# Low parts of half B's weights on VectorE, its conversions later in the order, and a list schedule that keeps GpSimd's arithmetic and VectorE's SBUF-only steps apart

## The chip, the cores and the metric

One core of a Trainium2 chip. The metric is the time of one execution on the device, in microseconds; the median of some runs counts. PE is TensorE, ACT is ScalarE, DVE is VectorE, POOL is GpSimd and SP is the engine that issues most DMAs.

## The reference

Attention over 4 batches and 8 heads of 576 x 64 with a threshold under the row's maximum, then two mixture layers on its 2304 x 512 output, with 2048 hidden units each:

```python
scores = scale * np.matmul(q, k.transpose(0, 1, 3, 2))
thresh = np.max(scores, axis=-1, keepdims=True) - tau
scores = np.where(scores >= thresh, scores, -1000000000.0)
attn = np.exp(scores - np.max(scores, axis=-1, keepdims=True))
attn = attn / (np.sum(attn, axis=-1, keepdims=True) + 1e-09)
x = np.matmul(attn, v)                    # -> 2304 x 512
h = x @ moe_w_in;  g = h * np.clip(h + 3.0, 0.0, 6.0) / 6.0
x = g @ moe_w_out
h = x @ moe2_w_in; g = h - np.tanh(h)
out = g @ moe2_w_out
```

The mixture weights arrive as 64-bit floats (two 32-bit words for a number), so the kernel converts them itself.

## The kernel before

The matrix products of the mixture layers run as three passes over pairs of a high and a low part (`mm3`: high x high, high x low, low x high). Every weight tile therefore goes through a conversion, `load_w` (L334 to L383): a DMA on SP brings 512 KB into one of three `st` buffers (L351 for the in-weights, L356 for the out-weights); ACT takes the absolute value of the upper words (L359) into `wu` (or, for half A, into a PSUM buffer `m`: the argument `scratch`); DVE does four steps on it, L362 and L364 (one input each), L367 and L370 (two inputs each, 128 x 512); then `hi_lo` (L385) writes the high part on ACT (L388) and the low part by a subtraction on GpSimd (L391). An in-weight has two such pairs of 128 x 256, an out-weight one of 128 x 512. The `st` buffer is free for the next load once the low parts have been computed.

The program's stages: attention, on PE interleaved with layer 1 of the first mixture, half A of its hidden units (`layer1`: 8 calls of 256 or 320 tokens, weights resident); then half B of the first mixture (`hidden` and `second`, 9 blocks of 256 tokens, 8 hidden tiles m each, from 511 us on), for which 16 weights are loaded and converted by `load_w` (L935 to L941) while the attention ends; then the second mixture in two halves. In the attention DVE does a row maximum L597, a threshold product L608 and steps on q and k (L507, L500); `invert` (L675 and L678) makes the reciprocals by which GpSimd scales the attention's output (L688), before PE transposes it (L685) and ACT and DVE (L694, L696) make its high and low part, `xT`. In layer 1 a gate is ACT L706, DVE L708, ACT L713 and the low part L716 (on GpSimd for layer 1, on DVE for half B); the second product is L749. In half B a matmul group is 12 matmuls of 128 x 256, h or m by `hidden` and ya by `second`. GpSimd also issues the loads of half B's x (L905).

What sets the order is `Plan` (L62 to L169), a list scheduler that runs when the kernel is built. Each task has an engine, a modelled duration, a key and the tasks that it depends on. In model time each free engine takes, of the tasks whose inputs are there and whose ring buffers have a slot, the one with the smallest key. The order found is the order of each engine's instruction queue; on the chip each engine then runs its queue in order and waits on semaphores. The weights of half B have the key `start - FW + WBO + WBS * (2 * m + o)` for the load and that plus 3 and further steps for the conversion, with `WBO` = 0 and `WBS` = 1.8.

```python
end = free[e] = now + t.dur
if t.xfer or e == "dma":
    end = moving = max(moving, now + 1.3) + t.xfer
```

## Time and profile before

| | |
|---|---|
| median of 3 runs | 1117.58 us (1115.91 to 1121.68) |
| the profiled execution | 1115.07 us |
| its span in the profile | 1113.3 us |
| its mean granted TensorE clock | 0.968 of full speed |
| PE busy in the span | 1045.2 us (94%) |
| DVE busy | 826.1 us (74%) |
| ACT busy | 660.0 us (59%) |
| POOL busy | 377.1 us (34%) |

Busy time counts an engine as long as an instruction is in it, so that a DVE instruction which is held up counts as busy too. Matmuls overlap each other, and their ends are modelled. In the timelines the number in brackets is the time for which the engine was idle ahead of the instruction, and the name behind it is what ended that idle time. A clock of 1.00 is TensorE's upper level of 2.4 GHz.

### The profile page before, as it was taken

The page shows a single profiled execution, that of the slowest core. Times are in us where ns is not written, and L with a number is a line of the kernel's source. Part 1 is how long each engine was busy: PE and PEld are TensorE (multiplying, and loading weights), DVE is VectorE, ACT ScalarE, POOL GpSimd, SP SyncE. Part 2 cuts the span into 40 slices and gives each one's busy share as a digit, 9 for nine tenths or more (in the row PEclk, how much of TensorE's full clock was granted, in tenths as well). Part 3 has the DMA queues.
Part 4 walks back from the last instruction along what each step waited for, and adds up shares of the span by engine and source line. Part 5 has one row for each costly group of instructions (what it writes and reads, how often), then busy time and mean ns, then how long its engine had stood idle before and what let it go on. Part 6 is the DMA issues. An engine that isn't in the chain of part 4 may idle for free.

```text
span 1113.3 us, 23731 instructions
## 1 busy us (share of the span) xinstructions
PE 1045.2 (94%) x8912; PEld 974.5 (88%) x8912; DVE 826.1 (74%) x1737; ACT 660.0 (59%) x1420; POOL 377.1 (34%) x413
## 2 busy tenths in 40 slices
PE   5668799999999999989899999999999999999998
PEld 4556788998999899979899999988989888888887
DVE  6889877688778876758676776896796786656653
ACT  6877888688868876555443444654564564333332
POOL 3666757566756675586211100000000010010100
PEclk8669899999999999999899999999999999999999
DMA  7889678867987787868797764654732662643613
GB/s 187 174 210 212 132 189 159 189 133 190 163 171 144 175 141 146 183 198 256 204 293 232 240 196 166 236 181 142 265 132 86 224 202 77 190 132 79 199 46 95
DMA packets 283666, 193.96 MB, mean 174 GB/s; under 512 B 203424, under 2 KB 254112, under 8 KB 283552
## 3 DMA queue, kind: packets, MB, share of 16 engines
q1 hardware_dynamic: 268672, 166.50, 57.5%
q0 software_dynamic: 14256, 25.69, 8.1%
q8 instruction: 70, 1.15, 0.4%
q10 hardware_dynamic: 624, 0.26, 0.1%
q14 instruction: 44, 0.36, 0.1%
HBM read 96.99 MB, written 52.95 MB: 135 GB/s over the span
## 4 chain that ended last, share of the span: by engine, by line
PE 79%; DVE 9%; ACT 4%; DMA 3%; issue 3%; POOL 1%; SPq 0%; DVEq 0%; ACTq 0%; POOLq 0%
PE ya L403 26%; PE m L403 21%; PE h L403 10%; PE s L592 7%; PE m L749 7%; PE tp L643 5%; DVE e L608 2%; PE tp L475 2%; DMA pt<-pp 1%; DVE z L597 1%; DMA st<-in_moe_w_in_dram 1%; ACT e L599 1%; ACT pp L613 1%; POOL pp L617 1%; DVE st L370 1%
## 5 line engine op out<-in xcount | busy, mean ns | idle before, releaser
L403 PE MATMUL ya<-wo,g 128*128 128x512 f32 x864 | 238.0, 395 | 0.6 <-ACT g L713 0.3
L617 POOL TENSOR_TENSOR pp<-e,pp 128x128 f16<-128x128 f32 (+3 forms) x160 | 185.4, 1179 | 119.7 <-ACT pp L613 62.6
L403 PEld LDWEIGHTS m<-x,wi 128*128 128x128 f32 x1392 | 187.3, 189 | 12.5 <-ACT t L1118 0.3
L403 PE MATMUL m<-x,wi 128*128 128x256 f32 x1392 | 194.6, 281 | 0.1
L403 PEld LDWEIGHTS ya<-wo,g 128*128 128x128 f32 x864 | 146.7, 188 | 19.8 <-DVE wu L1164 0.9
L597 DVE TENSOR_REDUCE z<-s 128x1 f32<-128x576 f32 x144 | 108.3, 753 | 51.5 <-PE s L592 50.5
L403 PEld LDWEIGHTS h<-x,wi 128*128 128x128 f32 x1008 | 136.1, 191 | 7.8
L403 PE MATMUL h<-x,wi 128*128 128x256 f32 x1008 | 142.1, 283 | 0.0
L713 ACT ACTIVATE g<-t 128x256 fp32r<-128x256 f32 x216 | 89.4, 415 | 75.6 <-DVE t L1131 49.5
L608 DVE SCALAR_TENSOR_TENSOR e<-s,z,e 128x576 f32<-128x576 f32 x144 | 116.1, 811 | 15.6 <-ACT e L599 10.0
L716 DVE TENSOR_TENSOR g<-t,g 128x256 fp32r<-128x256 f32 x216 | 94.8, 440 | 42.7 <-ACT g L713 38.2
L403 PE MATMUL m<-xT,ai 128*128 128x256 f32 (+1 forms) x768 | 120.8, 303 | 2.7 <-DVE t L708 1.5
L592 PE MATMUL s<-ks,q 128*128 128x288 f32 x512 | 105.1, 334 | 17.7 <-DVE e L608 17.1
L403 PE MATMUL ya<-g,wo 128*128 128x256 f32 x864 | 116.3, 284 | 3.8 <-DVE g L716 3.2
L599 ACT ACTIVATE e<-s,z 128x576 f32<-128x576 f32 x144 | 105.3, 738 | 23.1 <-DVE z L597 18.2
L1130 ACT ACTIVATE t<-t 128x256 f32<-128x256 f32 x128 | 53.4, 417 | 106.3 <-DVE t L1123 105.7
L403 PEld LDWEIGHTS ya<-g,wo 128*128 128x128 f32 x864 | 109.1, 192 | 4.7 <-DVE g L716 3.8
L403 PEld LDWEIGHTS m<-xT,ai 128*128 128x128 f32 x768 | 107.3, 191 | 4.8 <-DVE t L708 2.2
L592 PEld LDWEIGHTS s<-ks,q 128*128 128x128 f32 x512 | 81.6, 210 | 25.1 <-issue 10.2
L643 PE MATMUL tp<-vt,pt 128*128 128x65 f16 (+1 forms) x2240 | 86.9, 198 | 8.2 <-DMA pt<-pp 3.8
L643 PEld LDWEIGHTS <-pt 128*128 128x128 f16 (+1 forms) x2240 | 78.6, 103 | 16.5 <-DMA pt<-pp 5.9
L613 ACT ACTIVATE pp<-e 128x1152 f16<-128x1152 f32 (+1 forms) x80 | 85.1, 1064 | 8.6 <-DVE e L608 8.2
(124 smaller groups left out, 1560.8 us busy)
## 6 DMA issues: line engine op xcount, KB each, us to landing
st<-in_moe_w_in_dram SPq DMA_DIRECT2D x32, 512.0 KB, 4.7
st<-in_moe_w_out_dram SPq DMA_DIRECT2D x32, 512.0 KB, 4.7
x<-xs POOLq DMA_DIRECT2D x36, 256.0 KB, 6.2
y<-y SPq DMA_DIRECT2D x18, 512.0 KB, 4.3
xs<-xT SPq DMA_DIRECT2D x8, 640.0 KB, 4.9
y<-ys SPq DMA_DIRECT2D x9, 512.0 KB, 5.0
po<-wu SPq DMA_DIRECT2D x18, 256.0 KB, 2.0
wu<-po SPq DMA_DIRECT2D x18, 256.0 KB, 2.8
```

The costliest lines, as they stand in the source:

```text
L403: nc.tensor.matmul(ps, l[a], r[b], start=first and t == 0 and i == 0, stop=last and t == 2 and i == n - 1,)
L592: nc.tensor.matmul(ps.t[:, half, 0:SH], l, ks[:, half * SH:(half + 1) * SH], start=i == 0, stop=i == len(ops) - 1,)
L597: add("dve", 0.69, key, lambda: nc.vector.tensor_reduce(out=z.t[:, 0:1], in_=s(), axis=AX.XY, op=ALU.max, negate=True), r=[ps], w=[z])
L599: exp = add("act", 0.66, key, lambda: nc.scalar.activation(out=ex(), in_=s(), func=ACTF.Exp, bias=z.t[:, 0:1]), r=[ps, z], w=[e])
L608: add("dve", 0.74, key, lambda: nc.vector.scalar_tensor_tensor(out=ex(), in0=s(), scalar=z.t[:, 1:2], in1=ex(), op0=ALU.is_ge, op1=ALU.mul ...
L613: high = add("act", t_act(w * S, sbuf=True), key, lambda: nc.scalar.activation(out=pp.t[:, 0:w, 0:S], in_=e.t[:, 0:w, :], func=ACTF.Copy), ...
L617: add("pool", t_pool(w * (src.stop - src.start)), key, lambda src=src, dst=dst: nc.gpsimd.tensor_tensor(out=pp.t[:, 0:w, dst], in0=e.t[:, ...
L643: nc.tensor.matmul(pv.t[0:m, w_ * (D + 1):(w_ + 1) * (D + 1)], pt.t[:, n, blk, rows], vv, start=o == 0, stop=o == len(ops) - 1)
L713: hi = add("act", t_act(n, sbuf=True), key, lambda: nc.scalar.activation(out=gh(), in_=t(), func=ACTF.Copy), r=[bt], w=[bh])
L716: add(low, t_pool(n) if low == "pool" else t_dve(n), key, lambda: eng.tensor_tensor(out=gl(), in0=t(), in1=gh().bitcast(F32), op=ALU.subtr ...
L749: prev = [add("pe", t_mm(n, 1), kd, lambda p=p, l=l, r=r, m=m, s=s, ps=ps: nc.tensor.matmul(ps.t[:, 0:n], W["o", m].t[:, l, s], r[m].t[:, ...
L1130: add("act", t_act(n), key, lambda: nc.scalar.activation(out=s_(), in_=h.t[:, 0:n], func=ACTF.Tanh), r=[h], w=[u])
```

## The change

Three things. First, a task has a new flag `port`: it is set for every task of GpSimd unless the call says otherwise, and for the DVE tasks that work on SBUF alone as the code has it: the conversion steps of `load_w` where they work in `wu` (half B and later weights), the low parts of `hi_lo` and `split`, and `invert`. The DMA issues of GpSimd are taken out of it. In model time, a flagged task of DVE lasts from when GpSimd's last flagged task has ended, and the other way round. Nothing is waited for on the chip by this; it changes the order that comes out. Second, the 24 low parts of half B's weights go from GpSimd to DVE (`WL = "dve"`). Third, the keys of half B's weights are 6 later (`WBO`) and 2.4 apart (`WBS`). `CB` and `CB1` are passed with 0, which was the default, and `YL`, which is dropped, was not used.

```diff
@@ class Plan, add and issue
-    def add(self, eng, dur, key, fn, r=(), w=(), after=(), xfer=0.0, hold=False, slack=0.0):
+    def add(self, eng, dur, key, fn, r=(), w=(), after=(), xfer=0.0, hold=False, slack=0.0, port=None):
...
-        t = Task(eng, dur, key, fn, deps, xfer, hold, slack)
+        t = Task(eng, dur, key, fn, deps, xfer, hold, slack, eng == "pool" if port is None else port)
...
+        port = {"dve": 0.0, "pool": 0.0}
...
-                end = free[e] = now + t.dur
+                end = free[e] = (max(now, port["pool" if e == "dve" else "dve"]) if t.port else now) + t.dur
+                if t.port:
+                    port[e] = end
@@ constants
-    T2O, WBO, WBS, YL, XL2 = 0.0, 0.0, 1.8, -20.0, 0
+    T2O, WBO, WBS, XL2 = 0.0, 6.0, 2.4, 0
     WBU = 8
+    WL, CB, CB1 = "dve", 0.0, 0.0
@@ load_w
-    def load_w(kind, m, src, key, step, to, after=(), slack=0.0, scratch=None, cs=0.0, first=None):
+    def load_w(kind, m, src, key, step, to, after=(), slack=0.0, scratch=None, cs=0.0, first=None, low="pool"):
...
-                r=[wu] if n < 2 else [wu, wst], w=[wst] if n == 3 and split_ else [wu], slack=cs)
+                r=[wu] if n < 2 else [wu, wst], w=[wst] if n == 3 and split_ else [wu], slack=cs, port=not scratch)
...
-            hi_lo(f32, W, [wst], key + 3 + 4 * step, step, n, cs)
+            hi_lo(f32, W, [wst], key + 3 + 4 * step, step, n, cs, low)
@@ hi_lo
-            out=put(1), in0=f32(), in1=put(0).bitcast(F32), op=ALU.subtract), r=[*r, W], w=[W], after=[hi], slack=cs)
+            out=put(1), in0=f32(), in1=put(0).bitcast(F32), op=ALU.subtract), r=[*r, W], w=[W], after=[hi], slack=cs, port=True)
@@ invert
-            add("dve", 0.4, key - 7.5, invert, r=[xt, sv], w=[rx])
+            add("dve", 0.4, key - 7.5, invert, r=[xt, sv], w=[rx], port=True)
@@ split
-            out=gl(), in0=t(), in1=gh().bitcast(F32), op=ALU.subtract), r=[bt], w=[bl], after=[hi])
+            out=gl(), in0=t(), in1=gh().bitcast(F32), op=ALU.subtract), r=[bt], w=[bl], after=[hi], port=True)
@@ the weights of half B
-                    [R_wi.new(), R_wi.new()] if kind == "i" else [R_wo.new()], late)
+                    [R_wi.new(), R_wi.new()] if kind == "i" else [R_wo.new()], late, cs=CB, first=CB1, low=WL)
```

`port=False` is added to the two places where GpSimd issues DMAs (`load_x` and the second mixture's x). In the changed file these lines stand 5 further down: L597 there is L602, L608 is L613, L362, L364, L367 and L370 are L367, L369, L372 and L375, L391 is L396, L708 is L713, L716 is L721 and L749 is L754.

The number at the start of a row below is its place in the engine's queue, with equal rows taken together.

The first place: DVE near the end of half A's conversions (`m`, `st`), among the attention's steps (L597, L608, L500) and layer 1's first gates (L708). Before:

```order
182 L370 SCALAR_TENSOR_TENSOR st<-st,m 128x512
183 L364 TENSOR_SCALAR m<-m 128x512
184 L608 SCALAR_TENSOR_TENSOR e<-s,z,e 128x576
185 L367 SCALAR_TENSOR_TENSOR m<-st,m 128x512
186 L608 SCALAR_TENSOR_TENSOR e<-s,z,e 128x576
187 L370 SCALAR_TENSOR_TENSOR st<-st,m 128x512
188 L500 TENSOR_TENSOR ks<-tp,ks 64x2x256 x2
189 L597 TENSOR_REDUCE z<-s 128x1
190 L500 TENSOR_TENSOR ks<-tp,ks 64x2x64
```

And now:

```order
173 L512 SCALAR_TENSOR_TENSOR q<-tp,tau_b,q 128x512
174 L369 TENSOR_SCALAR m<-m 128x512
175 L505 TENSOR_TENSOR ks<-tp,ks 64x2x256
176 L372 SCALAR_TENSOR_TENSOR m<-st,m 128x512
177 L613 SCALAR_TENSOR_TENSOR e<-s,z,e 128x576
178 L375 SCALAR_TENSOR_TENSOR st<-st,m 128x512
179 L713 SCALAR_TENSOR_TENSOR t<-t,m 128x256
180 L602 TENSOR_REDUCE z<-s 128x1
181 L505 TENSOR_TENSOR ks<-tp,ks 64x2x256
182 L613 SCALAR_TENSOR_TENSOR e<-s,z,e 128x576
```

The last L370 of half A stands at row 187 before and, as L375, at row 178 now. Steps of the softmax and gates that stood ahead of it stand behind it.

The second place: DVE in the last call of layer 1, whose gates are the 128x320 rows; the rows on `wu` and `st` convert weights of half B. Before:

```order
670 L708 SCALAR_TENSOR_TENSOR t<-t,m 128x320
671 L367 SCALAR_TENSOR_TENSOR wu<-st,wu 128x512
672 L362 TENSOR_SCALAR wu<-wu 128x512
673 L370 SCALAR_TENSOR_TENSOR st<-st,wu 128x512
674 L364 TENSOR_SCALAR wu<-wu 128x512
675 L708 SCALAR_TENSOR_TENSOR t<-t,m 128x320
676 L367 SCALAR_TENSOR_TENSOR wu<-st,wu 128x512
677 L362 TENSOR_SCALAR wu<-wu 128x512
678 L370 SCALAR_TENSOR_TENSOR st<-st,wu 128x512
679 L364 TENSOR_SCALAR wu<-wu 128x512
680 L708 SCALAR_TENSOR_TENSOR t<-t,m 128x320
681 L367 SCALAR_TENSOR_TENSOR wu<-st,wu 128x512
```

And now:

```order
656 L367 TENSOR_SCALAR wu<-wu 128x512
657 L369 TENSOR_SCALAR wu<-wu 128x512
658 L713 SCALAR_TENSOR_TENSOR t<-t,m 128x320
659 L372 SCALAR_TENSOR_TENSOR wu<-st,wu 128x512
660 L367 TENSOR_SCALAR wu<-wu 128x512
661 L713 SCALAR_TENSOR_TENSOR t<-t,m 128x320
662 L375 SCALAR_TENSOR_TENSOR st<-st,wu 128x512
663 L369 TENSOR_SCALAR wu<-wu 128x512
664 L713 SCALAR_TENSOR_TENSOR t<-t,m 128x320
665 L396 TENSOR_TENSOR wo<-st,wo 128x512
666 L713 SCALAR_TENSOR_TENSOR t<-t,m 128x320
667 L372 SCALAR_TENSOR_TENSOR wu<-st,wu 128x512
```

Of the conversion's steps between the gates, those from a later weight have moved behind the eighth gate (row 682 before, row 666 now), and a low part (L396) stands ahead of it.

The third place: DVE at half B's first gates (L708 or L713 with 128x256, on m and h in turn) and their low parts (L716 or L721). Before:

```order
700 L708 SCALAR_TENSOR_TENSOR t<-t,m 128x256
701 L362 TENSOR_SCALAR wu<-wu 128x512
702 L364 TENSOR_SCALAR wu<-wu 128x512
703 L716 TENSOR_TENSOR g<-t,g 128x256
704 L367 SCALAR_TENSOR_TENSOR wu<-st,wu 128x512
705 L362 TENSOR_SCALAR wu<-wu 128x512
706 L370 SCALAR_TENSOR_TENSOR st<-st,wu 128x512
707 L364 TENSOR_SCALAR wu<-wu 128x512
708 L708 SCALAR_TENSOR_TENSOR t<-t,h 128x256
709 L367 SCALAR_TENSOR_TENSOR wu<-st,wu 128x512
710 L716 TENSOR_TENSOR g<-t,g 128x256
711 L370 SCALAR_TENSOR_TENSOR st<-st,wu 128x512
```

And now:

```order
689 L713 SCALAR_TENSOR_TENSOR t<-t,m 128x256
690 L375 SCALAR_TENSOR_TENSOR st<-st,wu 128x512
691 L367 TENSOR_SCALAR wu<-wu 128x512
692 L721 TENSOR_TENSOR g<-t,g 128x256
693 L369 TENSOR_SCALAR wu<-wu 128x512
694 L396 TENSOR_TENSOR wi<-st,wi 128x256 x2
695 L372 SCALAR_TENSOR_TENSOR wu<-st,wu 128x512
696 L367 TENSOR_SCALAR wu<-wu 128x512
697 L375 SCALAR_TENSOR_TENSOR st<-st,wu 128x512
698 L369 TENSOR_SCALAR wu<-wu 128x512
699 L713 SCALAR_TENSOR_TENSOR t<-t,h 128x256
700 L396 TENSOR_TENSOR wo<-st,wo 128x512
```

From the first gate's L708 (row 700 and now row 689) to the second's (row 708 and row 699) there are 7 rows before and 9 now, with low parts of weights among them.

## Rows read from the trace of the kernel before

**Rows 1.** Stages: window, length, busy of PE, PEld, DVE, ACT, POOL; clock, DMA share.

```profile
84.00:136.00 52.00, 41.10 (x459) 36.52 (x457) 49.38 (x84) 44.05 (x95) 37.33 (x38) 0.89 0.80 175
136.00:470.00 334.00, 324.48 (x3683) 309.17 (x3682) 256.70 (x495) 258.83 (x496) 217.03 (x219) 1.00 0.81 165
470.00:545.00 75.00, 64.99 (x489) 62.60 (x488) 53.54 (x89) 38.17 (x84) 46.90 (x51) 0.93 0.75 217
545.00:1113.00 568.00, 562.42 (x3905) 522.43 (x3904) 399.17 (x953) 256.56 (x628) 30.87 (x52) 1.00 0.53 172
```

**Rows 2.** Timeline of PE, 129 to 141 us: start, duration, instruction, [idle before].

```profile
129.45 2.26 PE L592 MATMUL s<-ks,qs 128*128 128x288 f32 x8 [4.85 <-DVE e L608]
...
138.53 0.69 PE L592 MATMUL s<-ks,q 128*128 128x288 f32 x4
139.06 1.35 PE L749 MATMUL m<-gh,ao 128*128 128x256 f32 x10
140.25 1.03 PE L643 MATMUL tp<-vt,pt 128*128 128x65 f16 x28
```

**Rows 3.** Timeline of DVE, 101 to 104 us.

```profile
101.52 0.41 DVE L708 SCALAR_TENSOR_TENSOR t<-t,m 128x256 f32<-128x256 f32 x1
...
102.44 0.75 DVE L597 TENSOR_REDUCE z<-s 128x1 f32<-128x576 f32 x1
103.11 0.68 DVE L370 SCALAR_TENSOR_TENSOR st<-st,m 128x512 uint32<-128x512 uint32 x1
103.71 0.81 DVE L608 SCALAR_TENSOR_TENSOR e<-s,z,e 128x576 f32<-128x576 f32 x1
```

**Rows 4.** Timeline of PE in layer 1's last call, 476 to 499 us.

```profile
476.92 14.22 PE L403 MATMUL m<-xT,ai 128*128 128x320 f32 x84 [0.47 <-ACT xT L694]
492.10 2.02 PE L403 MATMUL m<-xT,ai 128*128 128x320 f32 x12 [0.95 <-DVE t L708]
496.17 1.29 PE L749 MATMUL m<-gh,ao 128*128 128x320 f32 x7 [2.05 <-DVE t L708]
497.66 2.17 PE L749 MATMUL m<-gh,ao 128*128 128x320 f32 x13 [0.20 <-DVE t L708]
```

**Rows 5.** Timeline of DVE beside it.

```profile
487.51 1.15 DVE L364 TENSOR_SCALAR wu<-wu 128x512 int32<-128x512 int32 x1
...
492.58 1.51 DVE L362 TENSOR_SCALAR wu<-wu 128x512 f32<-128x512 f32 x1
```

**Rows 6.** Timeline of POOL beside it.

```profile
487.51 0.87 POOL L716 TENSOR_TENSOR gl<-t,gh 128x320 fp32r<-128x320 f32 x1 [0.25 <-ACT gh L713]
```

**Rows 7.** Groups by line and shape, POOL, 440 to 700: busy us, mean ns.

```profile
L391 POOL TENSOR_TENSOR wi<-st,wi 128x256 fp32r<-128x256 f32 x16 | 13.5, 856 | 5.6 <-ACT wi L388 5.5
L391 POOL TENSOR_TENSOR wo<-st,wo 128x512 fp32r<-128x512 f32 x8 | 11.2, 1402 | 16.0 <-ACT wo L388 16.0
```

**Rows 8.** Groups by line and shape, DVE, 700 to 1113 us.

```profile
L391 DVE TENSOR_TENSOR wo<-c,wo 128x512 fp32r<-128x512 f32 x14 | 9.4, 684 | 0.2
...
L391 DVE TENSOR_TENSOR wi<-c,wi 128x256 fp32r<-128x256 f32 x24 | 9.4, 416 | 0.0
```

**Rows 9.** Timeline of PE at half B's start, 520 to 540 us.

```profile
520.33 1.58 PE L403 MATMUL ya<-g,wo 128*128 128x256 f32 x11 [0.55 <-DVE g L716]
...
523.86 3.00 PE L403 MATMUL ya<-g,wo 128*128 128x256 f32 x23 [0.40 <-DVE g L716]
...
534.60 0.39 PE L403 MATMUL ya<-g,wo 128*128 128x256 f32 x1 [0.60 <-ACT g L713]
537.23 2.71 PE L403 MATMUL ya<-g,wo 128*128 128x256 f32 x11 [2.25 <-DVE g L716]
```

**Rows 10.** One stage behind it; columns as in rows 1.

```profile
537.20:544.10 6.90, 6.87 (x36) 6.87 (x37) 6.38 (x11) 3.53 (x10) 3.13 (x4) 0.59 0.50 149
```

**Rows 11.** Chain of work that ended last: start, us, what.

```profile
523.55 10.01 DMA st<-in_moe_w_in_dram
```

**Rows 12.** DMA issues of the page: count, KB, median us to landing.

```profile
st<-in_moe_w_in_dram SPq DMA_DIRECT2D x32, 512.0 KB, 4.7
```

More of the change, by code (lines that the diff above doesn't have):

```diff
@@ L23, with __init__ @@
 class Task:
-    def __init__(self, eng, dur, key, fn, deps, xfer, hold, slack):
+    def __init__(self, eng, dur, key, fn, deps, xfer, hold, slack, port):
         self.eng, self.dur, self.key, self.fn, self.deps, self.xfer, self.hold = eng, dur, key, fn, deps, xfer, hold
-        self.slack = slack
+        self.slack, self.port = slack, port
 class Buf:
@@ L905, in load_x @@
                     add("pool", 1.0, key, lambda h=h, part=part, x=x: nc.gpsimd.dma_start(
-                        out=x.t[:, part, :, 0:n], in_=xs[:, part, 2 * h:2 * h + 2, c:c + n].bitcast(F32R)), w=[x], after=after)
+                        out=x.t[:, part, :, 0:n], in_=xs[:, part, 2 * h:2 * h + 2, c:c + n].bitcast(F32R)), w=[x], after=after, port=False)
             return xs_
@@ L1106, in again @@
                 add("pool", 1.0, key + i - 6.0, lambda x=x, name=name: nc.gpsimd.dma_start(
-                    out=x.t, in_=xd[p, name].bitcast(F32R)), w=[x], after=[stored, *after], xfer=1.6)
+                    out=x.t, in_=xd[p, name].bitcast(F32R)), w=[x], after=[stored, *after], xfer=1.6, port=False)
             return out
```

## The prediction

> **What bounds the kernel now.** I read the table of stages first. From 545 us to the end PE is busy 562.42 of 568 us, and from 136 to 470 us 324.48 of 334 [rows 1]: there only PE's own work counts, and the change leaves PE its instructions. PE idles mainly in two stages, 84 to 136 (10.9 us) and 470 to 545 (10.0 us), at granted clocks of 0.89 and 0.93 [rows 1]. In both it waits for DVE. So the question is how much of these two stages the new order gives back; a shift that is there at 545 is carried to the end one for one, since nothing behind it has slack to swallow it.
>
> Second, PE's timeline in those stages. At 129 us one wait of 4.85 us stands, released by DVE's e (L608) [rows 2]; DVE, shared by half A's conversions and the attention's softmax steps, runs without a gap in that stage, as from 101 to 104 us [rows 3]. In the last call of layer 1 there are waits of 0.95, 2.05 and 0.20 us on L708 [rows 4], and DVE's rows beside it show why: an L362 takes 1.51 us instead of some 0.4 [rows 5]. At half B's start there are waits of 0.55, 0.40, 0.60 and 2.25 us on g [rows 9].
>
> Third, what stretches DVE's rows: L364 needs 1.15 us at 487.51, exactly where GpSimd's gl (L716) of 0.87 us starts [rows 5, 6]. Half B's low parts (L391), which the change takes off GpSimd, take 856 ns (16 of them) and 1402 ns (8) there [rows 7]; the same shapes cost DVE 416 and 684 ns later in the program [rows 8].
>
> **The change, part by part.**
>
> *Low parts on DVE.* Added to DVE: 16 x 0.416 + 8 x 0.684 = 12.1 us, spread from layer 1's last call to half B's first two blocks. Removed: 24.7 us of GpSimd [rows 7], and with them what they stretch on DVE (the one L362 above lost 1.1 us). DVE is busy 53.54 of 75 us in the stage [rows 1], so its load hardly changes; what changes is which step stands ahead of which, and that no step goes through another engine's queue.
>
> *The last call of layer 1.* Between the fourth and the eighth gate (L708) DVE ran 11 conversion steps and runs 7 now, one of them a low part (second pair of order rows). Rows on DVE follow each other 0.08 us faster than they last (0.75 at 102.44, the next at 103.11, rows 3), so a one-input step of 0.41 us costs 0.33 and a two-input step of 0.68 us 0.60: 4 x 0.33 + 3 x 0.60 = 3.1 us. PE feeds those gates 2.0 us apart (84 matmuls of seven gates in 14.22 us, rows 4), so DVE keeps up. What is late next is the last gate's own chain through ACT and DVE, which the matmuls of the second product that can run ahead (7 in 1.29 us, rows 4) do not cover: of the 3.2 us of waits I leave 1.05. Against that, PE does the x transposes ahead of the last PV group now, by which layer 1's last call starts some 0.7 us later. Net 3.2 - 1.05 - 0.7 = **1.45 us gained**; bounds -0.7 (the waits stay) and 2.5 (they go).
>
> Here the Trainium skill (SBUF — State Buffer, Who interferes with whom) speaks against the change. The row first: L364 at 487.51 was held about as long as the GpSimd gl beside it took. The page's rule: a DVE instruction with two SBUF inputs, as each moved low part is, contends with a GpSimd instruction that reads SBUF, and whichever issues second waits for the whole of the first; the 1.15 us agree with such a hold. GpSimd keeps the eight gl of this call, so the low part ahead of the eighth gate could wait 0.87 us more, and by it the sum below would be 5.0 and not 5.9 us.
>
> *Half B's start.* Before: waits of 0.55 + 0.40 + 0.60 + 2.25 = 3.8 us [rows 9], and the clock falls behind the longest: from 537.20 to 544.10 it is 0.59 [rows 10], which costs 6.9 x 0.41 = 2.8 us; 6.6 in all. Now the conversions come later (keys 6 us later, and 2.4 us apart instead of 1.8), so more of them stand between the first gates (third pair of order rows), but each finds DVE unstretched. The second gate of half B stands behind the first step of the eleventh weight, whose load stands behind layer 1's last y store on SP. Replaying the new order with the prices of rows 3 and 8 and a landing of 4.7 us [rows 12], I get 4.1 us of waits, most of it there and at the ninth gate, none of them long, so I let the clock stay. Net 6.6 - 4.1 = **2.5 us gained**; bounds 0 (a wait like the 2.25 stays and takes the clock down again) and 6.6.
>
> *Early, where half A is converted.* The flag on `invert` and on GpSimd's arithmetic reorders DVE from the first `invert` on. From there to half A's last conversion DVE has 68 instead of 77 instructions (the first pair of order rows is the end of that piece): 3 L597 (0.67 each), 4 L608 (0.73) and 3 L708 (0.33) fewer [rows 3], one L500 more, taken at an L597's 0.67. That is 2.0 + 2.9 + 1.0 - 0.7 = 5.2 us earlier on an engine without gaps. For it PE has done less when layer 1's second product (L749) begins: 12 score matmuls (four start 0.53 before the next row: 1.6) and two PV groups (1.03 less the same overlap of 0.16: 1.7) are still to do [rows 2], 3.3 us. Net **1.9 us gained**; bounds 0 (the softmax steps set aside are waited for later) and 6.9 (the 4.85 us wait goes whole, and with it most of what the slow clock costs, some 2 us). From 136 to 470 the order differs too, but PE idles only 9.5 of 334 us there [rows 1]: I take 0, give or take 3.
>
> Edits that cost nothing: ACT, SP and PE keep their instructions; `cs` and `first` get the zeros that they had; the DMA issues that are freed of the flag behave as before it.
>
> Sum: 1.45 + 2.5 + 1.9 = 5.9 us. Against the profiled execution that is 1115.07 - 5.9 = 1109.2. The median of the runs lies 2.5 us above the profiled one: 1117.58 - 5.9 = **1111.7 us**. Half a per cent, about what a measurement of this kernel can tell from no change, is 5.6 us: the limits are 1112.0 and 1123.2, and the forecast lies just beyond the first.
>
> **The rivals.**
>
> A, *the early wait goes whole.* For it: DVE sets 5.2 us aside, against a wait of 4.85 us. Against: what PE waits for there is one of the softmax steps, and it is those that are put back. It gives 6.9 + 1.45 + 2.5 = 10.9 us, **1106.7**.
>
> B, *nothing net: the flag binds the model and not the chip.* GpSimd and DVE meet as before wherever the model's times are off, the early reorder trades one wait for another, and half B's gates wait behind conversions as they did. For it: DVE's load is the same, and gates stand behind conversions in both orders. Some 1.5 us gained, **1116**.
>
> C, *slower: DVE's queue stands behind late weight loads.* DVE takes its rows in order, and half B's gates stand between conversion steps. Before, one load landed after 10.01 us [rows 11], where the median is 4.7 [rows 12]. GpSimd's x loads (L905), free of the low parts that stood ahead of them, can start earlier, beside weight loads 11 to 14. A load that lands at 10.0 puts 5.3 us on every gate behind it, and such a wait brings the 2.8 us of slow clock: one such load gives 1117.6 - 5.9 + 5.3 + 2.8 = 1119.8, within the half per cent, two give **1125.1**. It decides (a loss of 5.9 + 5.6 = 11.5 us) from two loads at 9.1 us: 2 x 4.4 + 2.8 = 11.6. Against: the keys are further apart now, and only one load took that long.
>
> **How the numbers follow.** Chances: forecast 0.50, A 0.17, B 0.20, C 0.13. The forecast's terms do not reach their bounds together; at half of them it runs from about 1106 to 1117, so it falls on both sides of 1112.0: 0.28 faster, 0.22 same. A is faster, B same, C slower: faster 0.45, same 0.42, slower 0.13. The range for 8 in 10 takes in the forecast, most of A, all of B, and C's case of a single load: 1104 to 1121.
>
> **What would show it.** Right: the 4.85 us wait near 129 shrinks by some 2 us or comes after the first L749; the three waits on L708 in layer 1's last call come to about 1; L362 and L364 take about 0.4 us there, L367 and L370 0.68; half B starts near 509 and not 511; no stretch near 540 has a clock of 0.6; from 545 on the same times, shifted. Wrong: a DVE idle of several us for ACT's wu (L359) with a gate behind it (C); conversion steps as long as before (B); a new wait between 136 and 470, where I took 0; or a shift that is given back after 545.

## The result, and where the time went

The change makes the kernel slower. Before: 1116.67 us median of 6 runs (1115.53 to 1121.68). Now: 1129.2 us median of 6 runs (1125.99 to 1132.38). The ratio is 1.0106 with a 95% interval of 1.0079 to 1.0132. The profiled execution took 1125.99 us, with a span of 1124.2 us; before it was 1115.07 and 1113.3.

To find the stage, I cut both traces at the same pieces of work and not at the same times: the start of layer 1's last call (its first 128x320 matmul on PE) and the start of half B (the first matmul on x). The rows are of the same kind as [rows 1]: window, length, busy time and instructions of PE, PEld, DVE, ACT and POOL, then PE's clock. Before:

```profile
84.00:476.92 392.92, 369.49 (x4211) 348.95 (x4208) 308.97 (x587) 305.36 (x597) 257.44 (x259) 0.99 0.80 165
476.92:510.87 33.95, 30.74 (x193) 29.81 (x194) 23.15 (x33) 18.77 (x40) 26.88 (x30) 0.95 0.79 226
510.87:1113.00 602.13, 592.76 (x4130) 551.96 (x4128) 426.67 (x1000) 273.48 (x666) 47.81 (x70) 0.99 0.54 175
```

After:

```profile
84.00:493.17 409.17, 378.83 (x4203) 357.47 (x4201) 306.15 (x584) 307.30 (x596) 256.22 (x258) 0.95 0.78 158
493.17:525.01 31.84, 29.07 (x192) 28.28 (x193) 21.67 (x42) 17.36 (x37) 13.67 (x16) 1.00 0.81 232
525.01:1124.00 598.99, 591.00 (x4130) 549.64 (x4128) 427.46 (x1016) 275.55 (x669) 36.56 (x59) 1.00 0.54 177
```

PE does the same work in each pair of rows (the counts differ by a few, since some records of matmuls are missing). From 84 us to the last call it needs 409.17 us instead of 392.92: **16.25 us are lost there**. The last call takes 31.84 instead of 33.95 us, 2.1 us less; from half B to the end it is 599 instead of 602 us, 3.1 us less. 16.25 - 2.1 - 3.1 = 11.05, against 10.9 between the spans. So the two terms of the forecast that concern the tail came out near their size in this pair of profiles, and everything went wrong in the attention.

The first row also tells of what kind the loss is. PE's idle time there is 409.17 - 378.83 = 30.3 us instead of 23.4, 6.9 us more. The other 9.3 us are PE's busy time, 378.83 instead of 369.49 us for the same matmuls: their clock is 0.95 instead of 0.99.

The stages of [rows 1], now:

```profile
84.00:136.00 52.00, 36.90 (x342) 32.84 (x341) 42.38 (x72) 38.05 (x78) 30.25 (x30) 0.79 0.75 165
136.00:470.00 334.00, 322.28 (x3628) 306.25 (x3627) 250.88 (x490) 259.31 (x498) 215.15 (x218) 0.98 0.79 157
```

From 84 to 136 the clock is 0.79 instead of 0.89, and DVE is busy 42.38 of 52 us instead of 49.38: it idles 9.6 us where it idled 2.6. This is the engine of which I had said that it runs without a gap. What happens at the start of that stage is seen in PE's timeline. Before:

```profile
88.90 1.05 PE L685 MATMUL tp<-ident,x 128*128 128x128 f32 x4 [1.49 <-DVE qs L507]
...
91.46 1.06 PE L685 MATMUL tp<-ident,x 128*128 128x128 f32 x4
...
95.90 1.20 PE L403 MATMUL m<-xT,ai 128*128 128x256 f32 x8
```

After:

```profile
90.16 1.33 PE L597 MATMUL s<-ks,q 128*128 128x288 f32 x4 [3.62 <-DVE e L613]
...
96.04 2.62 PE L597 MATMUL s<-ks,q 128*128 128x288 f32 x8 [2.26 <-DVE e L613]
98.46 1.05 PE L690 MATMUL tp<-ident,x 128*128 128x128 f32 x4
101.34 1.09 PE L690 MATMUL tp<-ident,x 128*128 128x128 f32 x4 [1.83 <-DVE xT L701]
...
105.35 1.39 PE L408 MATMUL m<-xT,ai 128*128 128x256 f32 x8
```

An x transpose is four matmuls of L685, and layer 1's first call needs two. Before, the first of them stood ahead of these score matmuls and the second behind four, and layer 1's first matmul (L403, xT) ran at 95.90. Now 20 score matmuls stand ahead of them; those wait 3.62 and 2.26 us for DVE's e, and the transposes (L690) wait behind them, to 98.46 and 101.34. Their inputs had been ready for long, as GpSimd's timeline shows (L693 scales the attention's output, which is what is transposed):

```profile
83.90 1.04 POOL L693 TENSOR_TENSOR x<-x,rx 128x512 f32<-128x512 f32 x1 [0.46 <-DVE rx L683]
...
89.04 1.04 POOL L693 TENSOR_TENSOR x<-x,rx 128x512 f32<-128x512 f32 x1
```

The second of these ends at 90.08. Layer 1's first matmul is at 105.35, 9.45 us later (in the seven profiles that have the old order here it is at 95.7 to 97.7), and until then PE lacks the matmuls that filled its waits before. DVE, for its part, waits for what PE and ACT have not done:

```profile
86.39 0.70 DVE L367 TENSOR_SCALAR m<-m 128x512 f32<-128x512 f32 x1 [1.43 <-ACT m L364]
...
89.29 0.82 DVE L613 SCALAR_TENSOR_TENSOR e<-s,z,e 128x576 f32<-128x576 f32 x1 [0.93 <-ACT z L607]
...
130.01 0.68 DVE L375 SCALAR_TENSOR_TENSOR st<-st,m 128x512 uint32<-128x512 uint32 x1
```

The first conversion step (L367) waits 1.43 us for ACT, the maximum behind it (L602) waits with it, and the last of half A's conversions (L375) is at 130.01, where it was at 130.92 before: 0.9 us earlier, not 5.2. Even the 0.9 us isn't the order's: the first `invert`, up to which both queues are the same, ran at 83.27 instead of 84.53 us in this profile. Counted from it, the last conversion comes after 46.7 us, and before after 46.4.

What the forecast meant to move is layer 1's second product (L749, now L754). Before:

```profile
135.57 2.16 PE L749 MATMUL m<-gh,ao 128*128 128x256 f32 x16
```

After:

```profile
137.94 1.10 PE L754 MATMUL m<-gh,ao 128*128 128x256 f32 x7
```

It begins 2.4 us later, with the 3.3 us of PE's work that the prediction counted still to do: some 5.7 us are lost by then (in profiles of one order this start differs by 2 us). The other ten or so are lost behind it. Layer 1 has for each of the four batches a call of 256 tokens and one of 320, and the start of the latter (its first 128x320 matmul on PE) is a mark that every trace has. It comes 16.5, 13.7, 14.3 and 16.3 us later than before in the four batches, so that most is lost in the first batch (work around these calls has moved too, so the marks are rough). Ahead of that call PE's queue again has x transposes and score matmuls that wait for DVE. In the first batch one such wait, 1.97 us for DVE's e, ends at 171.33, and from 171 to 177 us PE's clock is 0.50, where before it was 1.00 from 136 to 470 us.

### The profile page after: what moved, and what is told of

The parts are those of the page before. It is cut to its first block, busy times and chain, and to the rows that moved or that the text cites. A ratio compares the mean times of both kernels' runs of the same rounds, so it can differ in the third digit from the quotient of the medians.

```text
span 1124.2 us, 23703 instructions
## 1 busy us (share of the span) xinstructions
PE 1051.0 (93%) x8912; PEld 978.8 (87%) x8912; DVE 823.5 (73%) x1761; ACT 663.0 (59%) x1420; POOL 352.7 (31%) x389
## 4 chain that ended last, share of the span: by engine, by line
PE 82%; DVE 7%; ACT 4%; DMA 3%; issue 2%; SPq 1%; POOL 0%; ACTq 0%; DVEq 0%; POOLq 0%
PE ya L408 26%; PE m L408 22%; PE h L408 10%; PE m L754 9%; PE s L597 7%; PE tp L648 6%; DVE e L613 2%; PE tp L480 1%; DVE z L602 1%; DMA st<-in_moe_w_out_dram 1%; DMA st<-in_moe_w_in_dram 1%; ACT e L604 1%; ACT pp L618 1%; DMA wdo<-wu 1%; PE tp L690 1%
## 5 line engine op out<-in xcount | busy, mean ns | idle before, releaser
L602 DVE TENSOR_REDUCE z<-s 128x1 f32<-128x576 f32 x144 | 108.0, 754 | 52.5 <-PE s L597 52.1
L613 DVE SCALAR_TENSOR_TENSOR e<-s,z,e 128x576 f32<-128x576 f32 x144 | 116.2, 811 | 21.3 <-ACT e L604 11.1
L597 PE MATMUL s<-ks,q 128*128 128x288 f32 x512 | 107.2, 339 | 21.4 <-DVE e L613 20.7
L721 DVE TENSOR_TENSOR g<-t,g 128x256 fp32r<-128x256 f32 x216 | 91.0, 422 | 40.5 <-ACT g L718 36.6
L597 PEld LDWEIGHTS s<-ks,q 128*128 128x128 f32 x512 | 84.0, 215 | 28.9 <-DVE e L613 12.7
L648 PE MATMUL tp<-vt,pt 128*128 128x65 f16 (+1 forms) x2240 | 90.4, 201 | 8.2 <-ACT m L364 2.2
L648 PEld LDWEIGHTS <-pt 128*128 128x128 f16 (+1 forms) x2240 | 81.4, 105 | 16.6 <-issue 8.5
```

What stands on the lines that cost most here:

```text
L597: nc.tensor.matmul(ps.t[:, half, 0:SH], l, ks[:, half * SH:(half + 1) * SH], start=i == 0, stop=i == len(ops) - 1,)
L602: add("dve", 0.69, key, lambda: nc.vector.tensor_reduce(out=z.t[:, 0:1], in_=s(), axis=AX.XY, op=ALU.max, negate=True), r=[ps], w=[z])
L613: add("dve", 0.74, key, lambda: nc.vector.scalar_tensor_tensor(out=ex(), in0=s(), scalar=z.t[:, 1:2], in1=ex(), op0=ALU.is_ge, op1=ALU.mul ...
L648: nc.tensor.matmul(pv.t[0:m, w_ * (D + 1):(w_ + 1) * (D + 1)], pt.t[:, n, blk, rows], vv, start=o == 0, stop=o == len(ops) - 1)
L721: add(low, t_pool(n) if low == "pool" else t_dve(n), key, lambda: eng.tensor_tensor(out=gl(), in0=t(), in1=gh().bitcast(F32), op=ALU.subtr ...
```

## The experiments

All comparisons are with the kernel before on the same chip. The start of layer 1's last call differs by up to 3 us among seven profiles whose queues are the same up to shortly before it (476.7 to 479.9 us), so no smaller shift of a single start is read; for these the timed ratios count.

### Which part of the change loses, and which gains

The early order changes only because `invert` has the flag. Two kernels split the change there.

```diff
-            add("dve", 0.4, key - 7.5, invert, r=[xt, sv], w=[rx], port=True)
+            add("dve", 0.4, key - 7.5, invert, r=[xt, sv], w=[rx])
```

> The change without the flag on invert; the order up to about 430 us is then that of the kernel before. Theory T: all that was lost (half B starts 14.1 us later) was lost in the attention, by the order that the flagged invert sets off, while the last call of layer 1 gained 2.1 us and half B's start 3.2. So 1116.7 - 5.3 = about 1111.5. Rival R1 (the loss belongs to low parts and conversions on DVE, and the early order is innocent): still about 1127.

Measured: 1113.3 us (1110.9 to 1115.41, 6 runs) against 1118.34; ratio 0.9953 (0.9937 to 0.9969). A second time, with more rounds:

> The change without the flag on invert, a second time, with more rounds and beside the next kernel: 4 to 6 us below before if the first result was not an accident of a chip.

Measured: 1113.27 us (9 runs) against 1117.65; 0.9964 (0.995 to 0.9977). So the change without that one flag is **faster than both kernels**. Its stages up to the last call, and the last call:

```profile
84.00:479.88 395.88, 372.24 (x4221) 351.56 (x4219) 308.86 (x588) 305.92 (x597) 256.99 (x259) 0.98 0.79 164
479.88:511.84 31.96, 30.44 (x193) 29.82 (x194) 21.83 (x42) 17.51 (x37) 13.72 (x16) 0.95 0.80 231
```

The attention takes 395.88 us, within the spread of before's 392.92, and the last call 31.96, as in the change (31.97 in the profile of the second time). From half B to the end, though, these two profiles gain some 1.6 and 0.9 us, not the change's 3.1. The counterpart has the flag on `invert` and on GpSimd's arithmetic alone, with everything else as before (against the change; `split` likewise):

```diff
-    T2O, WBO, WBS, XL2 = 0.0, 6.0, 2.4, 0
+    T2O, WBO, WBS, XL2 = 0.0, 0.0, 1.8, 0
-    WL, CB, CB1 = "dve", 0.0, 0.0
+    WL, CB, CB1 = "pool", 0.0, 0.0
...
-                r=[wu] if n < 2 else [wu, wst], w=[wst] if n == 3 and split_ else [wu], slack=cs, port=not scratch)
+                r=[wu] if n < 2 else [wu, wst], w=[wst] if n == 3 and split_ else [wu], slack=cs)
...
-            out=put(1), in0=f32(), in1=put(0).bitcast(F32), op=ALU.subtract), r=[*r, W], w=[W], after=[hi], slack=cs, port=True)
+            out=put(1), in0=f32(), in1=put(0).bitcast(F32), op=ALU.subtract), r=[*r, W], w=[W], after=[hi], slack=cs, port=eng == "pool")
```

> The kernel before with the flag on invert and GpSimd's arithmetic alone; low parts on GpSimd, old keys, conversions without flag. T: the order up to about 430 us is that of the change, so its loss there is whole (last call of layer 1 begins some 16 us later) and the 5.3 us of gain are missing: 1131 to 1133. R1: about 1117, as before.

Measured: 1135.12 us (4 runs); 1.0146 (1.0126 to 1.0166), 16.8 us slower, 2 us beyond what T expected. The two results are on opposite sides of before and about add up to the change's own ratio (0.9953 x 1.0146 = 1.0098, measured 1.0106). R1 is out: the loss belongs to the order that the flagged `invert` sets off, the gain to the rest.

### The flag, or the order that it sets off

When the kernel is built, the scheduler holds the first `invert` for 0.95 us in model time, because a GpSimd task is then under way. Two kernels test whether that one hold is what counts, and whether anything but the order does.

```diff
-            add("dve", 0.4, key - 7.5, invert, r=[xt, sv], w=[rx], port=True)
+            add("dve", 0.4, key - 7.5, invert, r=[xt, sv], w=[rx], port=len(X1) > 1)
```

> The change, with only the first of the ten inverts without the flag. T, in its narrow form (the loss is made at the first invert, before 211 us, where 11 of the 16 us were lost): the first call of layer 1 begins near 96 us again, and the time is 1112 to 1116. Rival R2 (every flagged invert costs its share, 1 to 2 us each): 1125 or more.

Measured: 1118.7 us (10 runs); 1.001 (0.9995 to 1.0024). There are twelve `invert` tasks in the program, of which the change's schedule holds ten. Freeing the first gives back about 1%, so most of the loss hangs on it; but 0.5% is still missing against the kernel in which none has the flag. The narrow form of the theory (all of it at the first) is wrong by that.

Against the kernel before:

```diff
-            add("dve", 0.4, key - 7.5, invert, r=[xt, sv], w=[rx])
+            add("dve", 0.4 if len(X1) > 1 else 1.35, key - 7.5, invert, r=[xt, sv], w=[rx])
```

> The kernel before without any flag; only the modelled duration of the first invert is 1.35 instead of 0.4 us, which is by how much the flag held it in the scheduler's model. Nothing on the chip is another instruction; from that invert to about 200 us the order is that of the change. T: the loss of about 11 us by 211 us comes back, 1126 to 1129. R2, or any theory by which GpSimd and DVE meet differently on the chip because of the flag: 1117.

Measured: 1123.91 us (4 runs); 1.0059 (1.004 to 1.0079). No flag and no other instruction, only a number in a model that moves the queues' order, and 0.6% are lost; in its profile layer 1's first matmul is at 107.1 us. The loss is a little over half of what I expected. The queues of DVE and ACT are the change's up to 161 us, not to 200, and differ from there on; low parts and keys are the old ones.

### Late transposes, or any other order

If late transposes are what costs (T1), then holding them alone must cost, and an order that leaves them early must not. Against the kernel before:

```diff
-        add("pe", 0.00085 * KD * w, key, tr, r=[xt], w=[tp, xT])
+        add("pe", 0.00085 * KD * w, key, tr, r=[xt], w=[tp, xT], slack=1.0 if len(X1) == 1 and i == 0 else 0.0)
```

> The kernel before, no flag, every duration as it was; only PE's first x transpose of layer 1's first call is held 1 us later in the scheduler's model, and stands behind 20 score matmuls in PE's queue, as in the change; DVE's queue is that of before up to and past the first invert. Theory T1 (the loss comes from PE's transposes standing behind score matmuls that wait for DVE, so that layer 1's first call, which would fill PE, begins some 10 us late): the first layer-1 matmul near 107 us, the time 5 to 10 us above before. Rival T2 (DVE's conversions ahead of its softmax steps are what costs, set off by the held invert): within 2 us of before.

Measured: 1132.87 us (4 runs); 1.0139 (1.0118 to 1.016). More than T1 expected. DVE's `invert` stands where it stood, so a held `invert` isn't needed for such a loss. T2's other half, conversions ahead of softmax steps, isn't excluded: behind the first `invert` DVE's order has changed here too, with 65 instructions from it to half A's last conversion, where before has 77 and the change 68. PE's timeline:

```profile
97.57 2.62 PE L592 MATMUL s<-ks,q 128*128 128x288 f32 x8 [2.26 <-DVE e L608]
103.35 1.09 PE L685 MATMUL tp<-ident,x 128*128 128x128 f32 x4 [3.15 <-DVE ks L500]
...
118.17 1.11 PE L685 MATMUL tp<-ident,x 128*128 128x128 f32 x4 [0.68 <-DVE ks L500]
```

The first transpose (x, L685) runs at 103.35, the second at 118.17, and layer 1's first matmul only at 122.5. Up to the last call:

```profile
84.00:493.07 409.07, 378.88 (x4235) 356.69 (x4234) 311.42 (x589) 308.51 (x600) 258.73 (x261) 0.95 0.76 158
```

409.07 us, like the change's 409.17, with 30.2 us of idle time and the same clock of 0.95. But layer 1 began 27 us late here, not 9.45, and the loss has another course: 8.4 us by the first batch's call of 320 tokens (the table below), most of the rest between the second batch's and the third's. So late transposes go with a loss of about the size that T1 expected, in the first batch, and that the sums agree is a coincidence.

```diff
-            add("dve", 0.4, key - 7.5, invert, r=[xt, sv], w=[rx])
+            add("dve", 0.4 if len(X1) > 1 else 0.3, key - 7.5, invert, r=[xt, sv], w=[rx])
```

> The kernel before, no flag; the modelled duration of the first invert is 0.3 instead of 0.4 us. This also sets off another order from that place to about 250 us, but with both first x transposes ahead of the score matmuls. T1: no loss in the early stage, within 3 us of before. Rival R4 (the order of before is tuned, and any order set off by a small disturbance loses as much): 5 us or more above before.

Measured: 1125.71 us (4 runs); 1.0076 (1.0056 to 1.0096). T1 misses: here layer 1's first matmul is on time (97.4 us), and 8.6 us are lost all the same. The same with 0.2:

```diff
-            add("dve", 0.4, key - 7.5, invert, r=[xt, sv], w=[rx])
+            add("dve", 0.4 if len(X1) > 1 else 0.2, key - 7.5, invert, r=[xt, sv], w=[rx])
```

> The kernel before, no flag; the modelled duration of the first invert is 0.2 instead of 0.4 us. Another order again from that place, with PE's first x transpose even ahead of its place before. T1 (what costs is a late first call of layer 1): within 3 us of before, the miss of the run with 0.3 being an accident. R4 (orders set off by a small disturbance lose, wherever the transposes stand, because DVE and PE wait for each other in more places of the first batch): 4 us or more above before, with the first layer-1 matmul on time and more idle time on DVE between 84 and 136 us than the 2.6 us of before.

Measured: 1123.98 us (7 runs); 1.0055 (1.0035 to 1.0074). Slower again, as R4 says, but not for R4's reason. Layer 1's first matmul is at 93.7 us, 2 us earlier than before, and nothing is lost by 263 us. DVE idles 4.7 us from 84 to 136, but with the order of before it did so for 4.2 us in the profile of the kernel without the flag on `invert`. The loss comes later:

```profile
84.00:484.98 400.98, 376.37 (x4208) 356.20 (x4207) 310.50 (x587) 306.41 (x597) 256.64 (x259) 0.96 0.77 161
263.00:300.00 37.00, 34.60 (x323) 32.29 (x322) 29.64 (x63) 29.71 (x54) 26.15 (x27) 0.86 0.75 167
372.00:404.00 32.00, 27.88 (x309) 25.74 (x307) 27.29 (x55) 27.90 (x50) 24.96 (x24) 0.89 0.75 166
```

The same windows of before:

```profile
263.00:300.00 37.00, 34.90 (x374) 32.67 (x373) 31.44 (x65) 32.77 (x61) 28.57 (x29) 1.00 0.92 188
372.00:404.00 32.00, 29.99 (x318) 27.87 (x317) 27.80 (x59) 28.88 (x56) 25.32 (x25) 1.00 0.84 173
```

From 263 to 300 PE idles 2.4 us, against 2.1 before, and from 372 to 404 4.1 against 2.0. What differs is the clock, 0.86 and 0.89 where before it is 1.00: 37 x 0.14 + 32 x 0.11 = 8.7 us by the windows' lengths. Counted as for the change, by PE's busy time up to the last call, it is 376.37 - 369.49 = 6.9 of the 400.98 - 392.92 = 8.1 us that are lost (two profiles of the old order differ in this busy time by up to 2.8 us). The idle time is not alike in its spacing. PE's waits in the first window, with 0.2:

```profile
266.50 0.63 PE L685 MATMUL tp<-ident,x 128*128 128x128 f32 x4 [1.01 <-DVE xT L696]
...
268.53 1.70 PE L643 MATMUL tp<-vt,pt 128*128 128x65 f16 x28 [1.03 <-DVE xT L696]
```

Before:

```profile
265.69 1.01 PE L643 MATMUL tp<-vt,pt 128*128 128x65 f16 x28 [1.02 <-DVE xT L696]
```

With 0.2 two waits of 1 us for DVE's low part of x, `xT`, stand 2 us apart, and from the second of them on, 268 to 278 us, the clock is 0.50; before there is one, and the clock stays at 1.00, as it does from 136 to 470 us in the seven profiles that have this order. Both places lie ahead of a call of 320 tokens, as in the change. How much later than before that call starts, by batch, in us:

| profile | first | second | third | fourth |
|---|---|---|---|---|
| the change | 16.5 | 13.7 | 14.3 | 16.3 |
| the change without the flag on `invert` (order of before) | 2.0 | 1.8 | 1.8 | 3.0 |
| first `invert` 1.35 | 11.2 | 8.9 | 7.3 | 9.1 |
| first transpose held | 8.4 | 10.3 | 15.6 | 16.2 |
| first `invert` 0.3 | 5.0 | 8.3 | 8.7 | 10.9 |
| first `invert` 0.2 | 0.1 | 5.0 | 9.5 | 8.1 |

So T1 is one way to lose, in the first batch, and not the only one. PE waits for DVE's softmax steps and low parts of x in any of these orders; that of before gets through the later places at full clock, and this one doesn't. All four disturbances of the first place (this one, 0.3, 1.35 and the held transpose) lost 0.5% to 1.4%, so the order of before is better than these four neighbours; that none is as good isn't shown. That the clock falls where two waits come close together is seen at this place and not tested by a run; filling PE at those waits was not tried, and how much of the change's loss belongs to the late transposes stays open.

### What gains at the tail

With the early order of before, the parts of the rest were taken apart. Low parts on DVE and keys, no flag at all, against the change:

```diff
-                end = free[e] = (max(now, port["pool" if e == "dve" else "dve"]) if t.port else now) + t.dur
+                end = free[e] = now + t.dur
```

> The change without any flag: low parts of half B on DVE, with the later keys. The order up to about 430 us is that of before. If the low parts and the keys are what gained the 5 us of the kernel without the flag on invert alone: 4 to 6 us below before. If it was the flag on the conversions: within 2 us of before.

Measured: 1115.61 us (12 runs); 0.9981 (0.9969 to 0.9993). By the ratio that is 2.1 us, by the medians 1.5: at the edge of the second answer, and under half of the gain.

The flag on conversions and GpSimd alone, against the kernel without the flag on `invert`:

```diff
-    T2O, WBO, WBS, XL2 = 0.0, 6.0, 2.4, 0
+    T2O, WBO, WBS, XL2 = 0.0, 0.0, 1.8, 0
-    WL, CB, CB1 = "dve", 0.0, 0.0
+    WL, CB, CB1 = "pool", 0.0, 0.0
```

> The flag without invert, on the conversions of half B and GpSimd's arithmetic; low parts on GpSimd and the old keys. If the flag on the conversions made the gain: 3 to 5 us below before, and DVE's stretched rows (an L362 of 1.5 us, an L370 of 1.8 us in the kernel before) are gone. If the low parts on DVE and the keys made it: within 2 us of before.

Measured: 1118.58 us (12 runs); 1.0013 (1.0001 to 1.0026). The flag alone gains nothing, and the stretched rows are not gone: from 440 to 600 us L362 (here L367) takes 580 ns and L370 (L375) 885 ns in the mean, against 609 and 938 before. Flag and low parts on DVE with the old keys, against the same:

```diff
-    T2O, WBO, WBS, XL2 = 0.0, 6.0, 2.4, 0
+    T2O, WBO, WBS, XL2 = 0.0, 0.0, 1.8, 0
```

> The change without the flag on invert and with the old keys of half B's weights (0 and 1.8). If the later keys belong to the gain (theory: they leave fewer conversion steps ahead of the last gates of layer 1): 0 to 2 us below before. If the keys don't matter: 4 to 6 us below before, like the kernel with the new keys.

Measured: 1120.73 us (10 runs); 1.0031 (1.0016 to 1.0045). Neither answer: this is slower than before. The keys are worth 0.67% here, more than the whole gain. And the keys by themselves, against the kernel without any flag:

```diff
-    WL, CB, CB1 = "dve", 0.0, 0.0
+    WL, CB, CB1 = "pool", 0.0, 0.0
```

> The kernel before with only the later keys of half B's weights (6 and 2.4); low parts on GpSimd, no flag. The early order is that of before. The old keys cost the kernel with flag and low parts on DVE 7.5 us, so if the keys are the gain by themselves: 3 to 5 us below before. If they pay only together with low parts on DVE (whose queue is what they thin out): within 2 us of before.

Measured: 1115.83 us (12 runs); 0.9993 (0.9983 to 1.0002), no difference. So the gain is none of the three parts by itself: beside the flag, low parts on DVE pay only if the conversions come later. That the flag adds to them is likely and not shown: 0.9981 without it, 0.9953 and 0.9964 with it, and the intervals of the first and the last overlap. Low parts on DVE with the old keys and no flag were not tried. PE's timeline shows what the keys do. With the old ones (flag and low parts on DVE):

```profile
496.46 3.21 PE L408 MATMUL m<-xT,ai 128*128 128x320 f32 x12 [2.52 <-DVE t L713]
...
537.47 0.38 PE L408 MATMUL ya<-g,wo 128*128 128x256 f32 x1 [3.52 <-ACT g L718]
```

and with the new ones (the change without the flag on `invert`):

```profile
495.46 2.02 PE L408 MATMUL m<-xT,ai 128*128 128x320 f32 x12 [1.36 <-DVE t L713]
...
498.52 2.33 PE L754 MATMUL m<-gh,ao 128*128 128x320 f32 x14 [0.16 <-ACT gh L718]
...
529.88 0.39 PE L408 MATMUL ya<-g,wo 128*128 128x256 f32 x1 [2.07 <-ACT g L718]
```

The old keys leave a wait of 2.52 us on a gate of the last call and one of 3.52 us in half B; with the new ones these are 1.36 and 2.07 us.

## Why the prediction was wrong, point by point

**The early stage: 1.9 us gained, it said; 16.25 us were lost** up to the last call. This is the step that failed, in three places.

The first: "2.0 + 2.9 + 1.0 - 0.7 = 5.2 us earlier on an engine without gaps". The count of 68 instead of 77 instructions is right, the engine without gaps is not. That DVE idled only 2.6 us in [rows 1] was a property of the old order, in which PE and ACT always had something ready for it. Half A's last conversion came 0.9 us earlier in the trace and not at all counted from the first `invert`, and DVE idled 9.6 us.

The second: "for it PE has done less" counted what PE had still to do when L749 begins. It didn't look at what moved on PE's own queue ahead of that: the transposes went behind 20 score matmuls and took layer 1's first call, with which PE filled its waits for the softmax before, 9.45 us back. The rows of order that show it are PE's, and the prediction's are DVE's. "ACT, SP and PE keep their instructions" is true, but not their order. L749 began 2.4 us later, where the sum had it 5.2 earlier. The held transpose lost 8.4 us in the first batch with a call that began later still, so that an order with late transposes can cost this much; that they are the change's whole loss isn't shown.

The third: "From 136 to 470 the order differs too, but PE idles only 9.5 of 334 us there: I take 0, give or take 3". What idles little can come to idle more, and this is the larger part: of the 16.25 us some 10 were lost behind the start of L749. With the first `invert` free, a loss of 0.5% remained, and the `invert` of 0.2 lost all of its 8 us behind 263 us. Nor did the sum have a price for a clock that falls here: 9.3 of the 16.25 us are PE's busy time at a lower clock.

**The last call of layer 1: 1.45 gained (3.2 - 1.05 - 0.7); 2.1 us measured**, and that for another reason than the sum's, so by luck. The waits were to shrink from 3.2 to 1.05 us, and are 2.77:

```profile
505.40 2.02 PE L408 MATMUL m<-xT,ai 128*128 128x320 f32 x12 [1.40 <-DVE t L713]
508.63 2.02 PE L408 MATMUL m<-xT,ai 128*128 128x320 f32 x12 [1.21 <-DVE t L713]
...
511.69 2.33 PE L754 MATMUL m<-gh,ao 128*128 128x320 f32 x14 [0.16 <-ACT gh L718]
```

The other 1.7 us are the clock, 1.00 instead of 0.95 over the call. In the change without the flag on `invert` the call gained by its waits, as the sum had it: they are 1.36 and 0.16 us there, and the clock is 0.95 as before. What keeps DVE from the gates is seen on its own timeline:

```profile
503.40 0.43 DVE L367 TENSOR_SCALAR wu<-wu 128x512 f32<-128x512 f32 x1 [1.77 <-ACT wu L364]
503.86 1.09 DVE L369 TENSOR_SCALAR wu<-wu 128x512 int32<-128x512 int32 x1
...
507.31 0.43 DVE L367 TENSOR_SCALAR wu<-wu 128x512 f32<-128x512 f32 x1 [1.36 <-ACT wu L364]
...
510.09 0.71 DVE L396 TENSOR_TENSOR wo<-st,wo 128x512 fp32r<-128x512 f32 x1
```

It stands 1.77 and 1.36 us for ACT's wu, behind a weight that is late (ACT waited 1.60 and 2.47 us for `st` to land), with a gate behind it. That is the mechanism of rival C, with less than the 5.3 us that it had for one load, and one stage earlier. The 0.7 us for the transposes ahead of the last PV group were too little: the first of them waited 2.06 us for GpSimd, which is counted in the 16.25 us.

**The hold by GpSimd.** Here too L369 takes 1.09 us (503.86, above) beside a GpSimd instruction:

```profile
503.82 0.85 POOL L721 TENSOR_TENSOR gl<-t,gh 128x320 fp32r<-128x320 f32 x1 [1.85 <-ACT gh L718]
```

Like the prediction's L364, this row has one input in SBUF, and the rule that the prediction cites is on rows with two. The low part ahead of the eighth gate, which has two and by the rule could have waited 0.87 us, took 0.71 us (510.09), hardly more than the 684 ns of [rows 8]. That is no answer to the rule, since the gl that it met had 0.17 us left. With the old keys (flag and low parts on DVE) the same low part meets a gl that is under way:

```profile
496.99 1.08 POOL L721 TENSOR_TENSOR gl<-t,gh 128x320 fp32r<-128x320 f32 x1 [1.26 <-ACT gh L718]
```

```profile
497.27 1.35 DVE L396 TENSOR_TENSOR wo<-st,wo 128x512 fp32r<-128x512 f32 x1
```

It takes 0.67 us more than 684 ns, about the 0.80 us that the gl still has to run. There the rule (the Trainium skill, SBUF — State Buffer, Who interferes with whom) is seen. The flag did what it is for only in part. Over 440 to 600 us:

```profile
L367 DVE TENSOR_SCALAR wu<-wu 128x512 f32<-128x512 f32 x25 | 12.6, 503 | 12.9 <-ACT wu L364 12.4
L375 DVE SCALAR_TENSOR_TENSOR st<-st,wu 128x512 uint32<-128x512 uint32 x16 | 12.4, 781 | 0.1
...
L396 DVE TENSOR_TENSOR wi<-st,wi 128x256 fp32r<-128x256 f32 x16 | 6.1, 420 | 0.7 <-ACT wi L393 0.7
L396 DVE TENSOR_TENSOR wo<-st,wo 128x512 fp32r<-128x512 f32 x8 | 5.5, 694 | 0.5
```

L362 (now L367) is down from 609 to 503 ns and L370 (now L375) from 938 to 781 ns; before, from 600 us on, where GpSimd does little, L362 takes 432 and L370 684. The low parts cost DVE 420 and 694 ns, as [rows 8] said (416 and 684).

**Half B's start: 2.5 us gained; 3.1 measured.** The waits that [rows 9] showed with 3.8 us are now two:

```profile
542.79 0.39 PE L408 MATMUL ya<-g,wo 128*128 128x256 f32 x1 [1.81 <-ACT g L718]
543.61 1.56 PE L408 MATMUL ya<-g,wo 128*128 128x256 f32 x11 [0.43 <-DVE g L721]
```

2.24 us, where I had left 4.1, and the clock stays at 1.00 to 560 us, so that nothing answers to [rows 10]. That the sum comes near is in part luck: from half B to the end PE's busy time is 1.8 us less, where the clock was to give back 2.8, and what is left of the waits is 1.9 us less than the sum had, two misses of opposite sign.

**From 545 us on the shift is carried**: right. Half B starts 14.1 us later, the end comes 10.9 us later, and the difference is the gain at half B's start: from 560 us on PE stays 10.5 to 11 us behind.

**The rivals.** A: the early wait of 4.85 us did go (none over 2.1 us is left from 105 to 136 us), and more was lost elsewhere. B had the right thought, "the early reorder trades one wait for another", at the price of 0. C named the right side with the wrong place. What was missing among them is a rival in which the reordered attention loses: I had bounded that term by 0 from below, "the softmax steps set aside are waited for later", without a reason that excludes a loss.

## What to carry to other kernels

Where a list scheduler sets the order, a change of its model reaches every queue from the first task it touches on, and 0.95 us of model time at one small instruction cost 0.6% here without another instruction on the chip. Restrict a new rule to the stage for which it is meant, and compare the first rows that move on the engine that sets the time, not on the one that the rule is about. A stage in which an engine idles little is no bound on what another order can lose there; and parts that were tuned together (low parts and keys here) are worth something else apart.

## What the runs showed of the hardware

The clock made up more than half of the early loss (9.3 of 16.25 us of PE's time up to the last call) and most of it in the kernel with `invert` at 0.2 (6.9 of 8.1 us), in which PE's idle time was within 1.2 us of before's (24.6 against 23.4 us from 84 us to the last call). Between 263 and 300 us 2.1 us of idle time in one order left the clock at 1.00, and 2.4 us in another came with 0.86. Their sum doesn't tell what the clock will do; in this pair the clock fell at the second of two waits of 1.01 and 1.03 us that lay 2 us apart, where the other order has one of 1.02 us.

A subtraction on DVE with both inputs in SBUF (128x512, 684 ns by itself) took 1.35 us when it started 0.28 us behind a GpSimd subtraction of 1.08 us, and 0.71 us when it started 0.17 us before one ended.
